# Batch 5's exponentials moved one batch earlier and summed on GpSimd, in an attention and gated-FFN kernel

## The chip, the cores and the metric

One core of a Trainium2 chip. A time is the device time in microseconds (us) of one execution of the whole program. Engines are named as in the profile: PE is TensorE (PEld its weight loads), DVE is VectorE, ACT is ScalarE, POOL is GpSimd, SP is SyncE, which only issues transfers here.

## What is computed

Eight batches of attention with 8 heads, 576 positions and a head size of 64, compressed to 32 memory slots, and then a gated feed-forward block over all 4608 tokens:

```python
a = np.exp(phi - np.max(phi, axis=2, keepdims=True))          # phi: (8, 8, 576, 32)
a = a / (np.sum(a, axis=2, keepdims=True) + 1e-09)
k_m = np.einsum('bhsm,bhsd->bhmd', a, k)
v_m = np.einsum('bhsm,bhsd->bhmd', a, v)
scores = scale * np.matmul(q, k_m.transpose(0, 1, 3, 2))
attn = softmax(scores)                                         # over the 32 slots
x = np.matmul(attn, v_m)   # -> (4608, 512)
g = x @ w_gate             # 512 x 1536
out = (g * (1.0 / (1.0 + np.exp(-g))) * (x @ w_val)) @ w_out   # 1536 x 512
```

The change concerns the first two lines for one batch: the exponentials of phi and their sum over the 576 positions, the denominator of each of the 8 x 32 memory slots.

## The kernel before

All matmuls are in bfloat16 with float32 sums. The order of instructions on each engine is the order in which the program is written (a manual schedule); an engine takes its instructions one after the other and waits on semaphores. Batches 0 and 1 are a prologue; a loop runs over `b` from 2 to 7. One turn of the loop has two parts.

*Attention of b.* TensorE works off a backlog of output products of the batch before, six matmul units at a time (`run(take(6))`), and between them the scores of b (L396) are made. The products follow a seven-product scheme: four blocks of the hidden layer and their sums (`t_S`) are multiplied with blocks of the output weights and their sums (`t_T`), so that seven block products replace eight. They run in the order first, five, six, three, seven, four (L822), each with 12 matmuls (two per unit), and they accumulate in three PSUM banks called "s", "a" and "c" (in the profile p_os, p_oa, p_oc). Where a bank's sum is needed by itself and goes on being added to, `keep` (L744 to L750) copies it to SBUF on ScalarE: p5 from "c" (tile t_p) and q6 from "s" (tile t_q; the batch's q has a tile of the same name). ScalarE also takes the exponentials of the scores (L407) and, in the same stretch because the exponential's table is loaded there, the exponentials of the next batch's phi: `phi_exp(b + 1)` (L172, tile t_ephi, one instruction over 128 x 1152 elements). DVE computes the normalisation (L435 to L452) and writes the normalised attention t_A. Then ScalarE loads the table for silu (L1042).

*Gates of b.* TensorE makes 24 gate and 24 value products (L515, p_g and p_v), ScalarE the silu (L532), DVE the product of the two (L538, tile t_h). GpSimd makes sums of t_h (L603, L560, t_S), for the output products. Interleaved with the gates, TensorE prepares batch b + 1: the denominators (L258), the sums of k and v weighted by the exponentials (L230), and the values times the gate weights (L472).

The denominators go in one of two ways. `kv_denominators` multiplies with a matrix of ones either the nine blocks of t_ephi (nine products of 128 x 128 by 128 x 2), or, where `esums` has an entry for the batch, a high and a low bfloat16 part of their sum (two products). The sum is made by `phi_sum` on GpSimd at the head of the gates: it waits for the attention of the running batch through a one-element copy (`wait_for`, L645, t_mark), so that it doesn't start earlier, then does four additions (L212), a cast (L218) and a subtraction (L219). Batches 3, 4, 6 and 7 have such sums; batch 5 doesn't, since in the gates of batch 4 GpSimd works on `quad_sums(0)` (sums of the leftover rows of batches 0 to 3). In `kv_items`, a batch with sums other than 3 takes its denominators behind the k and v sums; batch 3, and batch 5 with its nine products, takes them ahead of these in a PSUM bank of their own (p_S).

Loads: `loads(b)` issues q, phi, k and v of batch b on GpSimd's queue, in this order. It is called for b + 3 from the gates of b, when the second of three chunks of t_h is done (`chunk_done`, L633). So the loads of batch 5 are issued in the gates of batch 2, and two phi tiles take turns. `load_qT` (SyncE's queue) then transposes q by a transfer, for batch 5 in the gates of batch 4.

The lines that fix the place of the exponential and of the sum in one turn of the loop, cut:

```python
        run(take(6))                # product five, ends with the copy p5
        if not last:
            phi_exp(b + 1)
        z_inv_v(b, 1)
        ...
        run(take(6))                # product six, ends with the copy q6
        run_late()
        ...
        nc.scalar.preload_act_table_set("silu_and_others")
        run(take(6))                # product three
        ...
        run(take(6))                # product seven
        ...                         # then the gates:
            if b != 4:
                phi_sum(b + 1)
```

Of the kernel before, what the change touches and what calls it, by code (L numbers as in the profile page):

```python
# [10 lines left out]
BF16 = mybir.dt.bfloat16  # L11
# [3 lines left out]
def kernel(  # L15
# [19 lines left out]
    nc = tc.nc  # L35
# [20 lines left out]
    att = ctx.enter_context(tc.tile_pool(name="att", bufs=2))  # L56
# [18 lines left out]
    def bank(shape, dtype, name):  # L75
        tag = free.pop(0)
        t = ps.tile(shape, dtype, tag=tag, name=name)
        held[id(t)] = tag, t
        return t

    def done(*tiles):

        for t in tiles:
            free.append(held.pop(id(t))[0])
# [3 lines left out]
    def head_pairs(x):  # L88

        return x.rearrange("h s d -> (h s d)").rearrange("(i p f) -> p i f", i=NP, p=128)  # L90

    def load_phi(b, eng):
        t = inp.tile([128, NP, JK * M], FP32, tag="phi", name="t_phi")
        eng.dma_start(out=t, in_=head_pairs(phi[b]))
        phis[b] = t
# [6 lines left out]
    def load_v(b):  # L102
        nc.gpsimd.dma_start(out=kvs[b][:, 1], in_=head_pairs(v[b]))  # L103

    def load_q(b):

        t = inp.tile([128, NS * 128], BF16, tag=f"q{Q_SLOT[b]}", bufs=1, name="t_q")
        nc.gpsimd.dma_start(  # L108
            out=t,
            in_=q[b].rearrange("h s d -> (h s d)").rearrange("(p f) -> p f", p=128),  # L110
        )
        qs[b] = t
# [55 lines left out]
    ephis, rSs, bkvs, kTs, es, atts = {}, {}, {}, {}, {}, {}  # L168

    def phi_exp(b):  # L170
        t = att.tile([128, JK, NP, M], BF16, tag="ephi", name="t_ephi")
        nc.scalar.activation(  # L172
            out=t.rearrange("p j i m -> p i j m"),
            in_=phis.pop(b).rearrange("p i (j m) -> p i j m", m=M),
            func=AF.Exp,
        )
        ephis[b] = t
# [24 lines left out]

    esums = {}

    def phi_sum(b):

        e = ephis[b].rearrange("p j i m -> p j (i m)")
        wait_for(atts[b - 1, 1][0:1, 0, 0:1])  # L210
        t = att.tile([128, 4, 128], FP32, tag="es", bufs=1, name="t_es")
        add = lambda o, x, y: nc.gpsimd.tensor_tensor(out=o, in0=x, in1=y, op=ALU.add)  # L212
        add(t, e[:, 0:4], e[:, 4:8])
        add(t[:, 0:2], t[:, 0:2], t[:, 2:4])
        add(t[:, 0], t[:, 0], t[:, 1])
        add(t[:, 0], t[:, 0], e[:, 8])
        hl = att.tile([128, 2, 128], BF16, tag="ehl", bufs=1, name="t_ehl")
        nc.gpsimd.tensor_copy(out=hl[:, 0], in_=t[:, 0])  # L218
        nc.gpsimd.tensor_tensor(out=hl[:, 1], in0=t[:, 0], in1=hl[:, 0], op=ALU.subtract)  # L219
        esums[b] = hl  # L220
# [18 lines left out]
    def kv_denominators(b, p):  # L239

        if b in masked:
            for g in range(NG):
                for j in range(JK):
                    nc.tensor.matmul(
                        p[:, g:g + 1],
                        lhsT=masked[b][:, j, g].rearrange("p i m -> p (i m)"),
                        rhs=ones1,
                        start=(j == 0),
                        stop=(j == JK - 1),
                    )  # L250
            return
        if b in esums:
            hl = esums.pop(b)
            terms = [hl[:, t] for t in range(2)]
        else:
            terms = [ephis[b][:, j].rearrange("p i m -> p (i m)") for j in range(JK)]
        for n, x in enumerate(terms):
            nc.tensor.matmul(p, lhsT=x, rhs=ones2, start=(n == 0), stop=(n == len(terms) - 1))  # L258

    def kv_reciprocal(b, p):  # L260
        r = att.tile([128, NG], FP32, tag="rS", name="t_rS")
        nc.vector.reciprocal(out=r, in_=p)
        rSs[b] = r
# [28 lines left out]
    def kv_items(b, beside=None):  # L292


        def run_sums():
            o = 2 * D
            behind = b in esums and b != 3
            own = beside and not behind
            if own:
                d = bank([128, NG], FP32, "p_S")  # L300
                kv_denominators(b, d)
                kv_reciprocal(b, d)
                done(d)
            p = [bank([128, CH], FP32, f"p_kv{g}") for g in range(NG)]
            if not (own or behind):
                kv_denominators(b, p[0][:, o:o + NG])
            kv_sum(b, p, (0, 1))
            if behind:
                beside()
                kv_denominators(b, p[0][:, o:o + NG])  # L310
            if not own:
                kv_reciprocal(b, p[0][:, o:o + NG])
            kv_norm(b, p)
            if beside and not behind:
                beside()

        return [run_sums, lambda: kv_T(b)]
# [324 lines left out]
    def wait_for(x):  # L642

        t = att.tile([1, 1], BF16, tag="mark", bufs=1, name="t_mark")
        nc.gpsimd.tensor_copy(out=t, in_=x)  # L645
# [331 lines left out]
    def loads(b):  # L977

        if b < B:
            load_q(b)  # L980
            load_phi(b, nc.gpsimd)
            load_k(b)
            load_v(b)

# [6 lines left out]
    for b in range(2, B):  # L991
        last = b + 1 == B
        exp_tables()
        if b == 2:
            load_qT(3)
            phi_exp(2)
            (zero, ops0), (one, ops1) = products(0, ("c11",)), products(1, ("p1", "c11"))
            kv, q2 = kv_items(2), q_items(2, "aaa")
            run(zero[:6])
            sums = {n: f for n, f in zip(((1, 1), (0, 2), (1, 2)), late)}  # L1000
            late.clear()
            sums[0, 2]()
            weight_sums(0)
            weight_sums(1)
            run(zero[6:12] + one[:6] + kv[:1] + q2[:2])
            weight_sums(2, (0, 1))
            run(zero[12:16] + q2[2:] + zero[18:22] + kv[1:] + zero[16:18] + zero[22:24])
            weight_sums(2, (2, 3))
            ops0["c11"]()
            ops1["p1"]()  # L1010
            wait_for(Ts[2][0:1, 3, 0, 0:1])
            for part in ((0, 1), (3,), (2,)):
                for c in (1, 2):
                    sums[1, c](part)
            loads(4)
            backlog = one[6:12] + zero[36:] + one[12:36]
            ops = ops1
        else:
            run(take(6))
        for g in range(NG):  # L1020
            scores(b, g)
        if b > 2:
            ops["p1"]()
            u_values(b)
        else:
            run(zero[24:36] + take(6))
        run(take(6))
        z_inv_v(b, 0)
        ops["c11"]()
        run(take(6))  # L1030
        if not last:
            phi_exp(b + 1)
        z_inv_v(b, 1)
        if b > 2:
            norm(b, 0)
            norm(b, 1)
        run(take(6))
        run_late()
        if b == 4:
            wait_for(atts[4, 1][0:1, 0, 0:1])  # L1040
            quad_sums(0)
        nc.scalar.preload_act_table_set("silu_and_others")  # L1042
        run(take(6))
        if b == 2:
            norm(2, 0)
        run(take(6))
        if b == 2:
            norm(2, 1)
            u_three(2)
            run(one[36:])  # L1050
        g = gv_slots(b)
        quad = []
        if b == 4:
            quad = products(b, (), 0)[0]
        if last:
            rest, rest_ops = products(b, (), 1)
            backlog += rest[:12]
        beside = 0 if last else 2 if quad else min(4, len(backlog))
        outs = [lambda: run(take(1)) for _ in range(len(backlog) - beside)]
        streams = [(g, 0, 24), (quad[:12], 0, 3), (quad[12:], 12, 18.5)]  # L1060
        streams += [(outs, 4, 7 if quad else 24)]
        if b == 2:
            streams += [([lambda: u_values(2)], 2.5, 3)]
        if last:
            streams += [([u_item(b, 2)], 5, 6)]
        if not last:
            if b > 2:
                load_qT(b + 1)
            if b != 4:
                phi_sum(b + 1)  # L1070
            streams += [
                (kv_items(b + 1, lambda: (u_item(b, 2, "aava")(), run(take(2)))), KV, KV + 4),
                ([lambda: (u_three(b + 1), run(take(2)))], 19, 20),
            ]
        spread(*streams)
        flush_mul()
        units, ops = products(b, ("p1", "c11"))
        backlog += units
# [34 lines left out]
```

## Time and profile before

| what | value |
|---|---|
| median of 3 runs | 232.76 us (232.63 to 233.4) |
| the profiled execution | 232.59 us, of which the span from first to last instruction is 230.8 us |
| granted TensorE clock in it | 1.0 |
| busy, share of the span | PE 96%, PEld 74%, DVE 80%, ACT 74%, POOL 63% |
| exponentials of phi on ScalarE (L172) | 6 of 1.16 to 1.17 us; batch 4's starts at 96.07 us, batch 5's at 119.92 us |
| denominators (L258) of batch 5 | 9 products from 128.53 us on |
| first sums of GpSimd in the gates of batch 3 | from 99.22 us on |
| loads of batch 5 | issued from 91.20 us on |

Times in the profile count from the first instruction. A line of a timeline gives the start, the duration, the engine, the line of the kernel, the operation, the tile written and those read, the shapes and how many instructions of a kind were merged; a bracket gives idle time of the engine before it and what ended it. Matmuls are pipelined, so their durations overlap: the distance from start to start is what one costs. "Landing" of a transfer is counted from the start of its issue.

### The profile page before, as it was taken

The numbers are of one execution on the slowest core, as the hardware profiler recorded it, in microseconds if no ns is written. First come the engines' busy times: TensorE is split into PE (matmuls) and PEld (weight loads), VectorE is DVE, ScalarE is ACT, GpSimd is POOL, SyncE is SP. The second block draws the span as 40 slices with busy tenths as digits, with TensorE's granted clock in tenths as the row PEclk, the third lists the DMA queues.
The fourth block names the chain that finished last, engine by engine and source line by source line (L and its number), as shares of the span: only waits on it lengthen the run. The fifth ranks groups of instructions, "written<-read, shape, count | busy, mean of one in ns | idle before, by whom it ended". The sixth has DMA issues, their size and how long they took to land.

```text
span 230.8 us, 7191 instructions
## 1 busy us (share of the span) xinstructions
PE 222.3 (96%) x2818; PEld 169.7 (74%) x2818; DVE 184.8 (80%) x423; ACT 171.6 (74%) x365; POOL 145.1 (63%) x197
## 2 busy tenths in 40 slices
PE   6997799999999999999999999999999999999993
PEld 2554476778887777878788787887788778878882
DVE  4056789999976799989997668998999899977832
ACT  2858898988547989968896658978898789677310
POOL 8422427998099759765977689464845394029291
PEclk9999999999999999999999999999999999999999
DMA  6999999999996993999299964996022602202024
GB/s 213 209 211 206 199 207 207 216 250 266 207 210 176 258 257 69 224 204 177 78 214 195 230 137 110 253 231 101 18 76 102 116 0 95 87 7 91 23 93 162
DMA packets 36546, 36.84 MB, mean 160 GB/s; under 512 B 14496, under 2 KB 30880, under 8 KB 36512
## 3 DMA queue, kind: packets, MB, share of 16 engines
q0 software_dynamic: 16272, 22.42, 52.7%
q1 hardware_dynamic: 19712, 13.37, 22.8%
q10 hardware_dynamic: 528, 0.59, 0.8%
q8 instruction: 22, 0.36, 0.6%
q14 instruction: 12, 0.10, 0.1%
HBM read 42.47 MB, written 9.44 MB: 225 GB/s over the span
## 4 chain that ended last, share of the span: by engine, by line
PE 87%; DMA 9%; POOL 2%; issue 0%; DVE 0%; POOLq 0%
PE p_os L723 21%; PE p_g L515 21%; PE p_v L515 20%; PE p_oc L723 10%; DMA W<-in_moe_w_val_dram 9%; PE p_oa L723 5%; PE p_u L472 5%; PE p_kv L230 2%; PE p_g L396 1%; POOL t_kv L99 1%; POOL t_kv L103 1%; PE p_q L383 1%; POOL t_q L108 0%; POOL W L138 0%; DVE t_q L339 0%
## 5 line engine op out<-in xcount | busy, mean ns | idle before, releaser
L538 DVE TENSOR_TENSOR t_h<-t_sg,p_v 128x288 bf16<-128x288 bf16 x192 | 81.7, 451 | 14.3 <-PE p_v L515 7.3
L515 PEld LDWEIGHTS <-t_U 128*128 128x128 bf16 x768 | 73.9, 98 | 21.2 <-issue 3.5
L532 ACT ACTIVATE t_sg<-p_g 128x288 bf16<-128x288 f32 x192 | 73.2, 424 | 17.2 <-PE p_g L515 11.4
L515 PE MATMUL p_g<-t_A,t_U 128*128 128x288 bf16 x384 | 77.0, 286 | 0.0
L515 PE MATMUL p_v<-t_A,t_U 128*128 128x288 bf16 x384 | 76.9, 286 | 0.0
L723 PEld LDWEIGHTS <-t_S 128*128 128x128 bf16 x384 | 37.3, 98 | 4.5 <-issue 0.2
L603 POOL TENSOR_TENSOR t_S<-t_h 128x512 bf16<-128x512 bf16 x17 | 19.6, 1154 | 27.7 <-DVE t_h L538 26.4
L723 PEld LDWEIGHTS <-t_h 128*128 128x128 bf16 x288 | 27.1, 98 | 8.6 <-issue 5.0
L492 ACT CAST t_U<-p_u 128x512 bf16<-128x512 f32 x51 | 27.0, 606 | 6.4 <-PE p_u L472 6.4
L723 PE MATMUL p_os<-t_T,t_S 128*128 128x256 bf16 x192 | 23.7, 273 | 0.0
L560 POOL TENSOR_TENSOR t_S<-t_S,t_h 128x512 bf16<-128x512 bf16 x17 | 19.6, 1155 | 1.3
L560 POOL TENSOR_TENSOR t_S<-t_h 128x512 bf16<-128x512 bf16 x16 | 18.4, 1152 | 0.0
L560 POOL TENSOR_TENSOR t_S<-t_h,t_S 128x512 bf16<-128x512 bf16 x16 | 18.4, 1151 | 0.0
L472 PE MATMUL p_u<-W,t_kT 64*32 64x512 bf16 (+1 forms) x416 | 15.3, 363 | 1.2 <-DMA W<-in_moe_w_val_dram 0.6
L870 PE MATMUL p_warm<-bones 128*128 128x512 bf16 x44 | 13.6, 450 | 1.7 <-DVE bones L892 1.7
L496 DVE CAST t_U<-p_u 128x512 bf16<-128x512 f32 x21 | 13.6, 683 | 1.9 <-PE p_u L472 1.9
L723 PE MATMUL p_os<-t_T,t_h 128*128 128x256 bf16 x96 | 14.8, 273 | 0.0
L452 DVE TENSOR_TENSOR t_A<-t_E,t_lz 128x576 bf16<-128x576 bf16 x16 | 11.4, 739 | 0.7 <-ACT t_lz L428 0.7
L723 PE MATMUL p_oc<-t_T,t_S 128*128 128x256 bf16 x96 | 11.9, 273 | 0.0
L723 PE MATMUL p_oa<-WO,t_h 128*128 128x256 bf16 x96 | 11.8, 273 | 0.0
L723 PE MATMUL p_oc<-WO,t_S 128*128 128x256 bf16 x96 | 11.8, 273 | 0.0
L723 PE MATMUL p_os<-WO,t_h 128*128 128x256 bf16 x96 | 11.8, 273 | 0.0
(108 smaller groups left out, 312.5 us busy)
## 6 DMA issues: line engine op xcount, KB each, us to landing
out_dram<-t_o SPq DMA_DIRECT2D x11, 512.0 KB, 3.3
t_kv<-in_k_dram POOLq DMA_DIRECT2D x8, 576.0 KB, 10.7
t_q<-in_q_dram POOLq DMA_DIRECT2D x8, 576.0 KB, 8.7
t_kv<-in_v_dram POOLq DMA_DIRECT2D x8, 576.0 KB, 15.1
t_phi<-in_phi_dram POOLq DMA_DIRECT2D x6, 576.0 KB, 8.5
out_dram<-t_o SPq DMA_DIRECT2D x10, 256.0 KB, 3.8
WO<-in_moe_w_out_dram POOLq DMA_DIRECT2D x3, 512.0 KB, 19.4
W<-in_moe_w_gate_dram POOLq DMA_DIRECT2D x2, 512.0 KB, 16.5
```

The source lines that it names most:

```text
L230: nc.tensor.matmul(p[g][32 * i:32 * i + 32, 0:n], lhsT=phi_of(b, g, j, i), rhs=kvs[b][64 * g:64 * g + 64, w0:w1, i, j * D:(j + 1) * D], st ...
L452: nc.vector.tensor_tensor(out=a, in0=es.pop((b, g)), in1=lzs.pop((b, g)), op=ALU.mult)
L472: nc.tensor.matmul(p[g][32 * i:32 * i + 32, o:o + n], lhsT=kTs[b][64 * g:64 * g + 64, 2, 32 * i:32 * i + 32], rhs=w_part(w, c, i, g, halve ...
L492: nc.scalar.copy(out=t, in_=p)
L496: nc.vector.tensor_copy(out=t, in_=p)
L515: nc.tensor.matmul(p[:, 0:HALF], lhsT=Us[b, c, g][:, o // 2, which, 128 * (o % 2):128 * (o % 2 + 1)], rhs=atts[b, g][:, r], start=(g == 0) ...
L532: nc.scalar.activation(out=sg, in_=gate[:, 0:HALF], func=AF.Silu)
L538: nc.vector.tensor_tensor(out=dst, in0=sg, in1=val[:, 0:HALF], op=ALU.mult)
L560: eng.tensor_tensor(out=out, in0=x, in1=y, op=ALU.subtract)
L603: eng.tensor_tensor(out=t[:, 0], in0=A21, in1=A22, op=ALU.add)
L723: nc.tensor.matmul(mine[home][:, u], lhsT=lhs(c, m, u), rhs=rhs(c, m), start=fresh and u == 0, stop=(k == 5), skip_group_check=u == 1 or n ...
L870: nc.tensor.matmul(p[:, 0:128 * a], lhsT=bones, rhs=x.to_broadcast([128, a, 128]) if a > 1 else bones, start=True, stop=True,)
```

## The change

The loop takes the exponentials of batches 4 and 5 in the attention of batch 3, one after the other, and none in the attention of batch 4. In the gates of batch 3 GpSimd makes the sums for batch 4 and then those for batch 5; both wait for the attention of batch 3 (`before`). The high and low parts get two buffers instead of one. Batch 5 keeps its place for the denominators (ahead of the k and v sums, in a bank of its own), which the test in `kv_items` now has to say, and takes two products there instead of nine. In the loads of batch 5, phi is issued ahead of q.

```diff
-    def phi_sum(b):
+    def phi_sum(b, before):
         e = ephis[b].rearrange("p j i m -> p j (i m)")
-        wait_for(atts[b - 1, 1][0:1, 0, 0:1])
+        wait_for(atts[before, 1][0:1, 0, 0:1])
...
-        hl = att.tile([128, 2, 128], BF16, tag="ehl", bufs=1, name="t_ehl")
+        hl = att.tile([128, 2, 128], BF16, tag="ehl", name="t_ehl")
...
         def run_sums():
             o = 2 * D
-            behind = b in esums and b != 3
+            behind = b in esums and b not in (3, 5)
...
     def loads(b):
         if b < B:
+            if b == 5:
+                load_phi(b, nc.gpsimd)
             load_q(b)
-            load_phi(b, nc.gpsimd)
+            if b != 5:
+                load_phi(b, nc.gpsimd)
             load_k(b)
             load_v(b)
...
         if not last:
-            phi_exp(b + 1)
+            for n in {3: (4, 5), 4: ()}.get(b, (b + 1,)):
+                phi_exp(n)
         z_inv_v(b, 1)
...
-            if b != 4:
-                phi_sum(b + 1)
+            for n in {3: (4, 5), 4: ()}.get(b, (b + 1,)):
+                phi_sum(n, b)
```

## The prediction

> **What bounds the kernel now.** I read the page first, for the engine that ends the run; then the timelines of ScalarE and TensorE around the place where the moved exponential lands (attention of batch 3); then TensorE at the denominators, GpSimd in the gates of batch 3, and the DMA issues ahead of the moved load.
>
> The page: busy time by engine, the granted clock, the chain that ended last.
>
> ```profile
> PE 222.3 (96%) x2818; PEld 169.7 (74%) x2818; DVE 184.8 (80%) x423; ACT 171.6 (74%) x365; POOL 145.1 (63%) x197
> PEclk9999999999999999999999999999999999999999
> PE 87%; DMA 9%; POOL 2%; issue 0%; DVE 0%; POOLq 0%
> ```
>
> TensorE carries 87% of the chain at a full clock, and the DMA part is the weight load at the start, which the change doesn't touch. From batch 2 on the program is a TensorE stream without holes: a window from 91.0 to 152.0 us shows it busy for all 61.0 us. So time taken out of that stream is won, and a hole put into it is lost; work on the other engines counts only where TensorE ends up waiting for it.
>
> ScalarE in the attention of batch 3 (start, duration, engine, line, operation):
>
> ```profile
> 95.59 0.58 ACT L748 COPY t_p<-p_oc 128x512 f32<-128x512 f32 x1 [0.26 <-PE p_oc L723]
> 96.07 1.17 ACT L172 ACTIVATE t_ephi<-t_phi 128x1152 bf16<-128x1152 f32 x1
> 97.14 0.58 ACT L748 COPY t_q<-p_os 128x512 f32<-128x512 f32 x1
> 97.73 1.28 ACT L1042 ACT_TABLE_LOAD   x1
> 99.77 0.41 ACT L532 ACTIVATE t_sg<-p_g 128x288 bf16<-128x288 f32 x1 [0.75 <-PE p_g L515]
> ```
>
> TensorE in the same stretch:
>
> ```profile
> 95.39 1.47 PE L723 MATMUL p_os<-t_T,t_S 128*128 128x256 bf16 x12
> 96.70 1.47 PE L723 MATMUL p_oc<-WO,t_S 128*128 128x256 bf16 x12
> 98.01 1.47 PE L723 MATMUL p_os<-t_T,t_S 128*128 128x256 bf16 x12
> 99.32 0.65 PE L515 MATMUL p_g<-t_A,t_U 128*128 128x288 bf16 x4
> ```
>
> These two belong together. The p_os of 95.39 is product six, the p_oc of 96.70 product three, the p_os of 98.01 product seven. Six and seven share one PSUM bank ("s"): `keep("q6", "s")` copies six out on ScalarE (t_q, 97.14 to 97.72) and only then may seven add into the bank. Today the copy ends 0.29 us before seven is due at 98.01. The exponential of L172 stands directly ahead of that copy in ScalarE's order.
>
> TensorE at batch 5's denominators (nine products, then the sums of k and v), and at batch 3's, which already has two products and the same bank of its own (p_S):
>
> ```profile
> 128.53 0.37 PE L258 MATMUL p_S<-ones,t_ephi 128*128 128x2 bf16 x9
> 128.83 0.80 PE L230 MATMUL p_kv<-t_kv,t_ephi 64*32 64x128 bf16 x72
> ...
> 79.84 0.19 PE L258 MATMUL p_S<-ones,t_ehl 128*128 128x2 bf16 x2
> 79.96 0.80 PE L230 MATMUL p_kv<-t_kv,t_ephi 64*32 64x128 bf16 x72
> ```
>
> Nine products hold the stream for 128.83 - 128.53 = 0.30 us, two for 79.96 - 79.84 = 0.12 us.
>
> GpSimd, from the loads of batch 5 to the first sums of batch 3's gates:
>
> ```profile
> 91.20 0.58 POOL L108 DMA_DIRECT2D t_q<-in_q_dram  x1
> 91.78 0.77 POOL L94 DMA_DIRECT2D t_phi<-in_phi_dram  x1
> ...
> 99.22 0.18 POOL L645 COPY t_mark<-t_A 1x1 bf16<-1x1 bf16 x1 [2.39 <-DVE t_A L452]
> 99.36 1.15 POOL L212 TENSOR_TENSOR t_es<-t_ephi 128x512 f32<-128x512 bf16 x1
> ...
> 102.79 0.43 POOL L219 TENSOR_TENSOR t_ehl<-t_es,t_ehl 128x128 bf16<-128x128 f32 x1
> 106.47 1.15 POOL L603 TENSOR_TENSOR t_S<-t_h 128x512 bf16<-128x512 bf16 x1 [3.25 <-DVE t_h L538]
> ```
>
> One phi_sum is 99.22 to 103.22, 4.0 us, and 3.25 us of idle follow it.
>
> DMA issues of that stretch (last number: us from issue to landing):
>
> ```profile
> t_q<-in_q_dram POOLq DMA_DIRECT2D x1, 576.0 KB, 5.4
> t_phi<-in_phi_dram POOLq DMA_DIRECT2D x1, 576.0 KB, 6.5
> ```
>
> Batch 5's q lands at 91.20 + 5.4 = 96.6, its phi at 91.78 + 6.5 = 98.3.
>
> **Part 1, seven products fewer.** Batch 5 goes from the p_S row with nine to the one with two: 0.30 - 0.12 = 0.18 us out of the stream, in the gates of batch 4. What follows (k and v sums, U, the casts on ScalarE at 129.89 that wait for TensorE) hangs on TensorE and moves along. Bounds: 0.18 gained, or nothing if a later wait eats it. I take 0.18. The two rows have weight loads of 95 to 98 ns each, yet the nine come about 25 ns apart.
>
> The Trainium skill, page "TensorE: Matmul & The Clock Gate", section "Back-to-back issue gap", says that small matmuls which each load weights are spaced by the weight load as well, about 81 ns at 128 columns; by that, as an estimate, seven products would be worth 0.57 us and the net below only +0.26. The nine products of this trace contradict it for this form, and I go by them.
>
> **Part 2, the second exponential.** It stands right behind the first, at 97.14, and takes ScalarE another 97.14 - 96.07 = 1.07 us from start to start. The copy t_q goes from 97.14 to 98.21 and ends at 98.79. Seven waits for it. A TensorE that stands waiting starts some 0.05 us after its releaser: DVE's copy of q ends at 13.00 + 1.23 = 14.23 and the waiting scores matmul starts at 14.28. So seven starts at 98.84 instead of 98.01: a hole of 0.83 us in the stream. Bounds: 0.78 with no release delay; 0.95 if the release takes three times as long.
>
> What stands behind the hole: gates of batch 3 move from 99.32 to 100.15. ScalarE's table load moves from 97.73 to 98.80 and ends at 100.08, while its first gate moves to 99.77 + 0.83 = 100.60, so the 0.75 us of idle there covers it. DVE's add that reads t_q (L753) starts at 99.01, after two norms, and finds t_q ready at 98.79. Everything later is paced by TensorE, so nothing gives the 0.83 back.
>
> In batch 4 the exponential is gone from ScalarE, but there the copy t_q (120.98 to 121.56) was in time for product seven at 121.85, and the first gate waits 0.97 us for TensorE: gain nothing.
>
> **Part 3, GpSimd.** The second phi_sum runs from 103.22 to about 107.2, where 3.25 us of idle were. The sums of batch 3 wait for t_h at 106.47, moved by the hole to 107.30: covered, cost nothing. Without the hole they would be 0.75 us late; the chain behind them has 0.37 us of idle at 117.33, and the last term that TensorE reads in batch 4 (ready at 119.69, read from 121.85) has over 2 us to spare. GpSimd at work beside DVE costs little: DVE's gate multiply takes 454 ns during the first phi_sum and 444 ns in the idle stretch after it, so perhaps four multiplies are 10 ns longer, 0.04 us at most and on an engine that TensorE does not wait for. The second mark waits for the same norm as the first, so it queues nothing new; the second ehl buffer removes a wait instead of adding one.
>
> **Part 4, the loads.** All four loads of batch 5 are still issued from 91.20 on. phi passes q: q lands no later than 98.3 instead of 96.6 and is wanted by the transposing load at 123.85, so it costs nothing; k and v keep their places. phi has to land before 97.14. First in the line, with q's 5.4 us from issue and 0.19 us more for its longer issue (0.77 against 0.58), it lands at 96.8 at the latest, 0.3 us in time; it moves half of q's source bytes, so sooner is likelier. Cost nothing, and one for one beyond 97.14.
>
> The Trainium skill, page "DMA: Bandwidth & Descriptors", section "Anatomy of one DMA — SWDGE (gpsimd) path", fits a GpSimd load as about 2.0 us plus bytes at 436 GB/s; as an estimate that is 3.4 us from the end of the issue and a landing at 95.3. The q row says up to 1.5 us later; by either the exponential is not held up and the sum stays.
>
> **Sum.** -0.18 + 0.83 = +0.65 us. On the profiled execution (span 230.8, time 232.59) that is 233.24; the median of the runs shown stands 0.17 higher at 232.76, and on it the forecast is 233.4.
>
> **The rivals.**
> A, the copy is not what seven waits for (another order on ScalarE, or slack that the trace doesn't show): only Part 1 is left, 232.6 on the median. For it speaks that the trace shows no wait of TensorE for t_q; against it that the slack is just 0.29 us and 1.07 us are put ahead of it on the same engine.
> B, clearly slower: phi of batch 5 lands late. If it lands at 98.3 as it does today, the exponential starts at 98.3 instead of 97.14, and the copy, product seven and all behind them move by another 1.2 us: +1.8 us, 234.6. It decides from 97.14 on; a landing at 97.5 would be +1.0. For it: the first packets of a set flow thinly for over a microsecond. Against: q, with twice the source bytes, lands at 96.6 from that place.
> C, the denominators stay nine: kv_denominators looks only at whether batch 5 has sums, so this would need the sums not to be built; 1% or so, and it would leave +0.83.
>
> **How the numbers follow.** Main case 80%: net between +0.60 (0.78 - 0.18) and +0.95 (the long release, nothing of Part 1 kept). About 0.3%, 0.70 us, is what a measurement of this kernel can tell from no change, and it cuts through this case: below it lie the sums that keep the 0.18, above it those that lose it; since the hole can hardly shrink while the gain can be lost, 37% below and 43% above. B 8%, slower. A 10%: 8% no difference, 2% faster. Of the remaining 2%, where ScalarE's relief in batch 4 is worth something that I can't see, I make faster too. Together faster 4%, same 45%, slower 51%. The range goes from A's side, 232.5, to B's landing at 97.9 (+1.4), 234.2.
>
> **What would show it.** After the change: two rows of L172 one behind the other near 96.1 and 97.1, t_q<-p_os near 98.2, and a hole of 0.8 us on TensorE ahead of the third p_os of batch 3, which the list of waits would give as L723 waiting for ScalarE's t_q L748; nine L258 rows on t_ephi left instead of eighteen; phi_sum twice back to back with the idle of 3.25 us gone. Wrong would be: seven still starting 1.31 us after three; or idle ahead of the second L172 ended by the DMA of t_phi.

## The result, and the profile after

The changed kernel takes 233.39 us (median of 20 runs, 233.22 to 234.32) against 232.69 us of the kernel before, timed beside it (20 runs, 232.44 to 233.4). The ratio is 1.0034, 95% interval 1.0027 to 1.0041: slower by 0.6 to 1.0 us. The profiled execution took 233.22 us with a span of 231.4 us; beside the profile of before that is 233.22 - 232.59 = +0.63 us.

The page after, the same three lines as before:

```profile
PE 222.1 (96%) x2811; PEld 169.3 (73%) x2811; DVE 185.1 (80%) x423; ACT 172.0 (74%) x365; POOL 148.9 (64%) x204
PEclk9999999999999999999999999999999999999999
PE 86%; DMA 9%; POOL 2%; ACT 1%; issue 1%; DVE 0%; POOLq 0%
```

Seven matmuls fewer on PE (2811 for 2818), seven instructions more on POOL (204 for 197: the six of a phi_sum and its mark), and ACT, which was not on the chain at all, now holds 1% of it. The busy lines alone would not tell that the kernel got slower: PE, the bound, has 0.2 us less work. What rose is its idle time.

ScalarE's timeline in the attention of batch 3, after:

```profile
95.59 0.59 ACT L748 COPY t_p<-p_oc 128x512 f32<-128x512 f32 x1 [0.26 <-PE p_oc L723]
96.08 2.22 ACT L172 ACTIVATE t_ephi<-t_phi 128x1152 bf16<-128x1152 f32 x2
98.20 0.57 ACT L748 COPY t_q<-p_os 128x512 f32<-128x512 f32 x1
98.79 1.28 ACT L1046 ACT_TABLE_LOAD   x1
100.57 1.64 ACT L532 ACTIVATE t_sg<-p_g 128x288 bf16<-128x288 f32 x4 [0.50 <-PE p_g L515]
```

TensorE's timeline in the same stretch, after:

```profile
95.39 1.47 PE L723 MATMUL p_os<-t_T,t_S 128*128 128x256 bf16 x12
96.70 1.47 PE L723 MATMUL p_oc<-WO,t_S 128*128 128x256 bf16 x12
98.82 1.47 PE L723 MATMUL p_os<-t_T,t_S 128*128 128x256 bf16 x12 [0.64 <-ACT t_q L748]
100.13 0.65 PE L515 MATMUL p_g<-t_A,t_U 128*128 128x288 bf16 x4
```

The copy t_q starts at 98.20 instead of 97.14, and product seven (the p_os of 98.82) now carries a bracket that it didn't have before: it waited for ACT's t_q. The bracket says 0.64, but the loss is 98.82 - 98.01 = 0.81 us: the bracket counts only from the modelled end of the last matmul, and matmuls overlap, so distances from start to start are what to read. The gates follow at 100.13 instead of 99.32.

The denominators of batch 5, after (the two rows of the k and v sums give the pace):

```profile
129.34 0.19 PE L258 MATMUL p_S<-ones,t_ehl 128*128 128x2 bf16 x2
129.46 0.80 PE L230 MATMUL p_kv<-t_kv,t_ephi 64*32 64x128 bf16 x72
```

129.46 - 129.34 = 0.12 us in place of 0.30. Laid start to start beside the trace of before, TensorE's stream is level to within 0.05 us from 27 us on until product seven, 0.81 us late from there on, and 0.63 us late from the k and v sums of batch 5 to the end of the program. There is no third step. (Ahead of 27 us lie the prologue's waits for loads, which end some tenths earlier or later from one execution to the next; they are level again by 27 us.)

GpSimd from the loads of batch 5 to the first sums of batch 3's gates, after:

```profile
91.21 0.79 POOL L94 DMA_DIRECT2D t_phi<-in_phi_dram  x1
92.00 0.55 POOL L108 DMA_DIRECT2D t_q<-in_q_dram  x1
...
103.17 0.18 POOL L645 COPY t_mark<-t_A 1x1 bf16<-1x1 bf16 x1
103.31 1.16 POOL L212 TENSOR_TENSOR t_es<-t_ephi 128x512 f32<-128x512 bf16 x1
...
107.28 1.16 POOL L603 TENSOR_TENSOR t_S<-t_h 128x512 bf16<-128x512 bf16 x1
```

The second phi_sum fills what was idle time, and the sums of batch 3 start at 107.28 with no idle ahead of them: they were due at 106.47 + 0.81. The DMA issues of that stretch, after:

```profile
t_phi<-in_phi_dram POOLq DMA_DIRECT2D x1, 576.0 KB, 4.3
t_q<-in_q_dram POOLq DMA_DIRECT2D x1, 576.0 KB, 6.2
```

phi landed at 91.21 + 4.3 = 95.5, 1.6 us before its exponential. In the traces of the experiments that load phi first it took 4.4 to 4.9 us and landed between 95.7 and 96.2, so at least 0.9 us ahead of 97.14.

### The profile page after: what moved, and what is told of

Read it like the earlier page. It is cut to its first block, busy times and chain, and to the rows that moved or that the text cites. A ratio compares the mean times of both kernels' runs of the same rounds, so it can differ in the third digit from the quotient of the medians.

```text
span 231.4 us, 7184 instructions
## 1 busy us (share of the span) xinstructions
PE 222.1 (96%) x2811; PEld 169.3 (73%) x2811; DVE 185.1 (80%) x423; ACT 172.0 (74%) x365; POOL 148.9 (64%) x204
## 4 chain that ended last, share of the span: by engine, by line
PE 86%; DMA 9%; POOL 2%; ACT 1%; issue 1%; DVE 0%; POOLq 0%
PE p_g L515 21%; PE p_v L515 20%; PE p_os L723 20%; PE p_oc L723 10%; DMA W<-in_moe_w_val_dram 9%; PE p_oa L723 5%; PE p_u L472 5%; PE p_kv L230 2%; ACT t_ephi L172 1%; PE p_g L396 1%; POOL t_kv L99 1%; POOL t_kv L103 1%; PE p_q L383 1%; POOL t_q L108 0%; POOL W L138 0%
## 5 line engine op out<-in xcount | busy, mean ns | idle before, releaser
L603 POOL TENSOR_TENSOR t_S<-t_h 128x512 bf16<-128x512 bf16 x17 | 19.7, 1156 | 24.5 <-DVE t_h L538 22.9
L560 POOL TENSOR_TENSOR t_S<-t_S,t_h 128x512 bf16<-128x512 bf16 x17 | 19.6, 1156 | 1.3
L560 POOL TENSOR_TENSOR t_S<-t_h,t_S 128x512 bf16<-128x512 bf16 x16 | 18.4, 1153 | 0.0
L560 POOL TENSOR_TENSOR t_S<-t_h 128x512 bf16<-128x512 bf16 x16 | 18.4, 1153 | 0.0
```

Source lines behind the costliest of these rows:

```text
L560: eng.tensor_tensor(out=out, in0=x, in1=y, op=ALU.subtract)
L603: eng.tensor_tensor(out=t[:, 0], in0=A21, in1=A22, op=ALU.add)
```

## The experiments

All take the changed kernel as their base, or the version of the first experiment, and were timed beside the kernel before.

### The exponential behind the copy

```diff
-        if not last:
-            for n in {3: (4, 5), 4: ()}.get(b, (b + 1,)):
-                phi_exp(n)
+        if not last and b != 4:
+            phi_exp(b + 1)
         z_inv_v(b, 1)
         ...
         run(take(6))              # product six, ends with the copy q6
+        if b == 3:
+            phi_exp(5)
         run_late()
```

> The changed kernel with one thing moved: batch 5's exponential stands behind the copy t_q (q6) on ScalarE in the attention of batch 3, not ahead of it. Sums on GpSimd, order of the loads and the two denominator products stay. Theory (the copy behind the second exponential holds product seven): t_q goes from 97.14 again, product seven starts at 98.01, no hole; the 0.18 us of the seven products stay won: 0.18 us under the kernel before, about 232.5, ratio 0.999. ScalarE's table load would end at 100.08, 0.31 us later than its first gate was due at 99.77; TensorE has free banks there, so I expect no wait of it. Rival (GpSimd's second phi_sum or the order of the loads costs the time, and the hole only lies where TensorE would have waited a little later anyhow): TensorE waits elsewhere in the gates of batch 3 or the attention of batch 4 and the time stays near +0.6 us.

Measured: 232.48 us (11 runs), ratio to before 0.999, interval 0.9981 to 0.9999. ScalarE, then TensorE, of this version:

```profile
96.15 1.17 ACT L172 ACTIVATE t_ephi<-t_phi 128x1152 bf16<-128x1152 f32 x1
97.21 0.58 ACT L748 COPY t_q<-p_os 128x512 f32<-128x512 f32 x1
97.68 1.18 ACT L172 ACTIVATE t_ephi<-t_phi 128x1152 bf16<-128x1152 f32 x1
98.87 1.28 ACT L1047 ACT_TABLE_LOAD   x1
100.17 1.80 ACT L532 ACTIVATE t_sg<-p_g 128x288 bf16<-128x288 f32 x5
```

```profile
96.78 1.47 PE L723 MATMUL p_oc<-WO,t_S 128*128 128x256 bf16 x12
98.08 1.47 PE L723 MATMUL p_os<-t_T,t_S 128*128 128x256 bf16 x12
99.39 0.65 PE L515 MATMUL p_g<-t_A,t_U 128*128 128x288 bf16 x4
```

Product seven follows three without a hole, and the gates follow seven. (Everything in this trace lies 0.07 us later than in the trace of before from 27 us on, behind the prologue's waits for loads; the distances count. From the denominators of batch 5 on it lies 0.10 us earlier, a gain of 0.17 us.) The first silu starts some 0.3 us after its gate was ready, right behind the table load, and TensorE doesn't notice. GpSimd's first sums start at 107.19, 0.65 us later than their operands were ready in the kernel before, and no wait of TensorE comes of it either. So the second phi_sum, the order of the loads and the later table load are free; the whole loss of the change is where the exponential stands. This version beats both kernels. Against before the medians differ by 0.30 us (the interval reaches from 0.02 to 0.44), the traces by the 0.17 us of the denominators.

### Nine products again, hole kept

```diff
-            for n in {3: (4, 5), 4: ()}.get(b, (b + 1,)):
+            for n in {4: ()}.get(b, (b + 1,)):
                 phi_sum(n, b)
```

> The changed kernel without the sums of batch 5 on GpSimd: the exponential stays moved, phi is still loaded first, and batch 5's denominators are nine products again. Theory: the hole ahead of product seven stays at 0.81 us and the 0.18 us of the denominators are not won: 0.8 us above the kernel before, 0.18 above the changed one, ratio about 1.0035. Rival (GpSimd's second phi_sum costs something): less than +0.6 us.

Measured: 233.67 us (5 runs), ratio 1.0037, interval 1.0024 to 1.0051. The median is 0.89 us above before; 0.81 was expected and lies in the interval, as do smaller values down to 0.56, so the times alone don't separate it from the changed kernel. The trace does: product three starts at 96.75 and seven at 98.87, the same hole of 0.81 us (98.87 - 96.75 - 1.31), and the nine products run from 129.73 to the k and v sums at 130.03, 0.30 us. So without the second phi_sum the hole is as long as with it. The profiled execution (233.79, the longest of the five) also has a second hole, in the gates of batch 3, with nothing that the profile could name as its cause:

```profile
105.38 0.41 PE L515 MATMUL p_v<-t_A,t_U 128*128 128x288 bf16 x2
105.97 0.42 PE L515 MATMUL p_g<-t_A,t_U 128*128 128x288 bf16 x2 [0.18 <-issue]
```

From start to start that is 0.59 instead of 0.25, 0.34 us lost. No other run's trace has it at this place. It says how far one profiled execution can be trusted where tenths matter, and is why the seven products were tested once more, in the fifth experiment.

### phi loaded second

```diff
     def loads(b):
         if b < B:
-            if b == 5:
-                load_phi(b, nc.gpsimd)
             load_q(b)
-            if b != 5:
-                load_phi(b, nc.gpsimd)
+            load_phi(b, nc.gpsimd)
```

> The changed kernel with the loads of batch 5 in the order of before: q, then phi. Theory: phi lands at about 98.3 (91.78 + 6.5) instead of 95.5, the second exponential starts there instead of at 97.14, the copy t_q ends at about 99.95 and the hole ahead of product seven grows from 0.81 to about 2.0 us: +1.8 us against before. Rival (ScalarE has slack there that the trace doesn't show): the hole stays at 0.8 us.

Measured: 234.61 us (2 runs), ratio 1.008, interval 1.0062 to 1.0098: +1.8 us. phi landed 6.6 us after its issue. ScalarE and TensorE of this version:

```profile
98.42 1.16 ACT L172 ACTIVATE t_ephi<-t_phi 128x1152 bf16<-128x1152 f32 x1 [1.19 <-DMA t_phi<-in_phi_dram]
99.49 0.57 ACT L748 COPY t_q<-p_os 128x512 f32<-128x512 f32 x1
```

```profile
96.70 1.47 PE L723 MATMUL p_oc<-WO,t_S 128*128 128x256 bf16 x12
100.11 1.47 PE L723 MATMUL p_os<-t_T,t_S 128*128 128x256 bf16 x12 [1.94 <-ACT t_q L748]
```

ScalarE now stands 1.19 us for the transfer, and the hole is 100.11 - 96.70 - 1.31 = 2.10 us. A wait on ScalarE passes to TensorE in full; the turned order of the loads in the change is what kept this from happening.

### One exponential more

```diff
         nc.scalar.activation(out=..., in_=..., func=AF.Exp)
+        if b == 5:
+            nc.scalar.activation(out=..., in_=..., func=AF.Exp)    # the same again
```

> The changed kernel with batch 5's exponential taken twice in a row into the same tile: one suspected cost doubled, nothing else. Theory: each exponential ahead of the copy t_q costs its 1.07 us from start to start one for one, so the hole ahead of product seven is 0.81 + 1.07 = 1.88 us and the time +1.7 us against before. The table load then ends at 101.15 and the gates start at 101.2, so it could add up to 0.1 us. Rival (part of the hole is a fixed cost of the wait, not the length of the exponential): the hole grows by clearly less or more than 1.07 us.

Measured: 234.51 us (2 runs), ratio 1.0076, interval 1.0057 to 1.0094: +1.7 us. ScalarE of this version (the lines behind the added exponential are numbered 7 higher in it):

```profile
96.19 2.22 ACT L172 ACTIVATE t_ephi<-t_phi 128x1152 bf16<-128x1152 f32 x2
98.44 1.16 ACT L178 ACTIVATE t_ephi<-t_phi 128x1152 bf16<-128x1152 f32 x1
99.51 0.57 ACT L755 COPY t_q<-p_os 128x512 f32<-128x512 f32 x1
```

TensorE's product three starts at 96.82 and seven at 100.13: a hole of 100.13 - 96.82 - 1.31 = 2.00 us, 1.19 more than with two exponentials. I had said 1.07. The third starts at 98.44, after the pair's end at 98.41, while independent ones overlap by 0.1 us (96.08 and 98.20 in the changed kernel hold two at 1.06 each). The third writes the tile that the second writes, and that it therefore waits for the second's end is inferred; the trace names no wait there. The second thus stands 1.18 us ahead of the third's start, and the hole grows by about that: what goes ahead of the copy costs its distance to the next start, and no fixed part shows.

### Sums made but not read

On the version of the first experiment:

```diff
-        if b in esums:
+        if b in esums and b != 5:
             hl = esums.pop(b)
```

> The version with batch 5's exponential behind the copy t_q, with GpSimd's sums for batch 5 still made but not read: batch 5's denominators are nine products again. It takes the two products away and leaves everything else. Theory (the gain of 0.18 us is the seven products and nothing else, and the sums, the loads and the later exponential are free): the time of the kernel before, ratio 1.000, and the denominators take 0.30 us of TensorE's stream again. Rival (the gain comes from ScalarE's relief in batch 4 or from the order of the loads): it stays 0.18 us or more under the kernel before.

Measured: 232.66 us (11 runs), ratio to before 0.9996, interval 0.9986 to 1.0005; 0.18 us above the first experiment's 232.48 us. TensorE at batch 5's denominators in this version:

```profile
128.66 0.37 PE L258 MATMUL p_S<-ones,t_ephi 128*128 128x2 bf16 x9
128.96 0.76 PE L230 MATMUL p_kv<-t_kv,t_ephi 64*32 64x128 bf16 x67
```

0.30 us again, and laid beside the first experiment's trace the stream falls 0.18 us behind exactly here and nowhere later. The seven products are the whole gain; the interval of either time taken alone would not show so small a thing, the step in the trace does.

### The two products behind the sums

On the version of the first experiment:

```diff
-            behind = b in esums and b not in (3, 5)
+            behind = b in esums and b != 3
```

> The version with batch 5's exponential behind the copy t_q, and batch 5's two products behind the sums of k and v like those of batches 4, 6 and 7, in the bank of the sums, not ahead of them in a bank of their own. Two products behind the sums took 0.06 us of the stream in batch 4 (104.22 to 104.28) against 0.12 us ahead of them in batch 3 (79.84 to 79.96). Theory: another 0.06 us, 0.24 us under the kernel before, ratio 0.999. Rival: DVE's reciprocal then comes later (behind the products instead of beside the sums), so the copies of the sums and their banks come later, and in the crowded gates of batch 4 TensorE waits for a bank: 0.1 to 0.3 us slower than the version without this.

Measured: 232.85 us (11 runs), ratio 1.0001, interval 0.9992 to 1.001: 0.37 us above the first experiment, the rival's direction and a little beyond its 0.1 to 0.3 us. Nor did the stretch of the sums get shorter: from the product ahead of them to the first gate behind them (128.34 to 130.35 here, 128.39 to 130.35 in the first experiment) the stream takes 2.01 us against 1.96, and in the gates that follow it falls another 0.35 us behind. TensorE, then DVE, of this version:

```profile
130.35 0.41 PE L515 MATMUL p_g<-t_A,t_U 128*128 128x288 bf16 x2
130.84 0.41 PE L515 MATMUL p_v<-t_A,t_U 128*128 128x288 bf16 x2
...
131.33 0.41 PE L515 MATMUL p_v<-t_A,t_U 128*128 128x288 bf16 x2
131.82 0.41 PE L515 MATMUL p_g<-t_A,t_U 128*128 128x288 bf16 x2
```

```profile
129.93 0.69 DVE L496 CAST t_U<-p_u 128x512 bf16<-128x512 f32 x1 [0.86 <-PE p_u L472]
130.54 0.16 DVE L262 RECIPROCAL t_rS<-p_kv 128x2 f32<-128x2 f32 x1
130.73 0.99 DVE L266 TENSOR_SCALAR t_bkv<-p_kv,t_rS 128x128 bf16<-128x128 f32 x4
131.64 2.37 DVE L538 TENSOR_TENSOR t_h<-t_sg,p_v 128x288 bf16<-128x288 bf16 x5
```

At two places (130.35 to 130.84 and 131.33 to 131.82) a pair of matmuls takes 0.49 us from start to start, instead of 0.28 and 0.24 in the first experiment. DVE copies the sums (L266) only from 130.73 on, because the reciprocal waits for the products; with the products ahead it does so from 129.58, while TensorE is still at other work. In this version DVE's first gate multiply behind them starts at 131.64, against 131.15. That TensorE stands for a bank which DVE has not freed is inferred from this order; the trace names no releaser for the two steps. Whatever the cause, the time speaks for the place ahead of the sums that the change keeps for batch 5's denominators.

### The sum for batch 5 made twice

On the version of the first experiment:

```diff
-            for n in {3: (4, 5), 4: ()}.get(b, (b + 1,)):
+            for n in {3: (4, 5, 5), 4: ()}.get(b, (b + 1,)):
                 phi_sum(n, b)
```

> The version with batch 5's exponential behind the copy t_q, with GpSimd's six instructions for batch 5's sum done twice: 3.95 us more on GpSimd, nothing else. In the version without this GpSimd runs without idle time from 99.3 to 118.9, so all 3.95 us pass on: the third sum of chunk 1 (made from 117.83 to 118.97) is ready at about 122.9 instead of 118.97. Product three of batch 3 reads it at its third unit, at about 120.8. Theory (GpSimd is hidden only by a cover of about 2 us in front of the products of batch 3): TensorE stands about 2.1 us ahead of that unit, and the time is about 234.6, +1.9 us against before. Rival (GpSimd has more room than that, or its sums are not what TensorE reads): the time stays at 232.5.

Measured: 234.81 and 236.38 us (2 runs; the second is the profiled one), ratio 1.012, interval 1.0081 to 1.016. TensorE of the profiled one:

```profile
120.52 0.60 PE L723 MATMUL p_oc<-WO,t_S 128*128 128x256 bf16 x4
123.31 1.89 PE L723 MATMUL p_oc<-WO,t_S 128*128 128x256 bf16 x8 [2.19 <-POOL t_S L560]
```

The third unit of product three was due four matmuls after the first, at 120.52 + 4 x 0.11 = 120.96, and started at 123.31: 2.35 us lost to the sum that GpSimd (L560, 122.11 + 1.14) had ready at 123.25. In the version with the single sum the same sum is ready at 117.83 + 1.15 = 118.98 and that unit starts at 121.06: the cover that hides GpSimd in batch 3 is 2.1 us there. The delay that used it up, 123.25 - 118.98 = 4.27 us, is larger than the 3.9 us that the doubled sum adds: GpSimd's three instructions from 116.00 on, which now stood beside sums on DVE (last section), took 3.14 us up to the next issue of a load, against 2.71 us in the first experiment. The run of 234.81 us is what the hole makes of 232.48; the other run lost 1.6 us more, which is told there too.

## Why the prediction was right

The forecast was 233.4 us with a net of +0.65; measured were 233.39 us, and +0.63 in the profile. That the time agrees to 0.01 us is luck: the forecast stood on the median of three runs of before, 232.76, which is 0.07 us above that of the 20 runs timed beside the change, and the medians differ by 0.70. The mechanism is what was right: the same two steps, at the places that were named, and no third.

- *Part 2, the second exponential*: 0.83 us forecast, 0.81 measured in the trace, at the instruction that was named and with the releaser that was named. The release delay is the forecast 0.05 us (the copy ends at 98.77, seven starts at 98.82); the difference of 0.02 is that the exponentials stand 1.06 us apart instead of 1.07 and the copy takes 0.57 instead of 0.58. The first experiment took the hole away by the order on ScalarE alone; the third and fourth made it grow with whatever is ahead of the copy.
- *Part 1, seven products*: 0.18 forecast, 0.18 measured, and the fifth experiment shows that nothing else contributes. The estimate of 0.57 us from the Trainium skill's page "TensorE: Matmul & The Clock Gate", section "Back-to-back issue gap", is not what these products cost: the nine come 25 ns apart with their weight loads. The page gives its 81 ns for products with 128 moving columns, and its table of single products has a floor of about 25 ns for 1 to 64 columns; these have 2, so the estimate took the wrong row.
- *Part 3, GpSimd*: free, as said, with the hole and without it. The margin was argued from the term that product seven reads; the last experiment shows TensorE waiting for product three's first, and in the first experiment's trace that one is the tightest, with 2.1 us. There, with GpSimd without a pause, product three's term is ready at 118.98 and read at 121.06, product seven's, the next sum that GpSimd makes, at 120.10 and read at 122.37, which leaves 2.3 us. The conclusion stood, the row behind it was not the one with the least room. The 10 ns allowed for each of DVE's gate multiplies did not appear either: the three that took 441 to 446 ns in the stretch without GpSimd took 443 to 446 ns beside the second phi_sum.
- *Part 4, the loads*: free, as said, with phi at 95.5. The bound from q's row (96.8) was 1.3 us too late; the estimate from the Trainium skill's page "DMA: Bandwidth & Descriptors", section "Anatomy of one DMA — SWDGE (gpsimd) path", 95.3, was the nearer of the two in this trace. The landings of the other traces with phi first, 95.7 to 96.2, lie between them. Rival B's price, +1.8 us, is what the third experiment measured with the loads turned back.
- *Rival A* (the copy is not what seven waits for) is refuted by the bracket on seven, and by the first experiment, which takes the hole away. *Rival C* didn't happen.
- *The cut at 0.3%* ran through the main case as said: +0.63 in the profile is 0.27%, the ratio of the runs 0.34%, and its interval reaches to both sides of 0.3%.

## What to carry to other kernels

Where, as here, an engine fed without holes is the bound, a piece of work moved on another engine does not cost its length as such, its place decides: look for the small instruction behind it that the bound waits for, and take the slack from the distance between the end of the one and the start of the other (here 0.29 us against 1.07 us put in front). Moving it one instruction further, behind that copy, turned a loss of 0.63 us into a gain of 0.17, by the traces. And a load that is consumed earlier than before has to be checked against its landing, not only its issue: without the turned order this change would have lost 1.8 us.

## What the runs showed of the hardware

Two things, both in the profiled run of the last experiment. The hole of TensorE cost more than its length there: the matmuls directly behind it came 0.21 us apart instead of 0.11, and the windows of that run show the clock beside them (stretch, its length, busy time and instructions of PE, PEld, DVE, ACT and POOL, granted clock, DMA share, GB/s):

```profile
120.50:123.30 2.80, 0.62 (x6) 0.30 (x4) 2.73 (x5) 1.87 (x2) 2.80 (x5) 0.99 0.93 155
123.30:126.80 3.50, 3.49 (x18) 2.51 (x19) 3.18 (x4) 0.00 (x0) 2.80 (x5) 0.52 1.07 283
126.80:130.00 3.20, 3.20 (x30) 2.73 (x28) 1.44 (x3) 1.51 (x4) 3.20 (x7) 1.00 1.18 183
```

For 3.5 us after the hole the granted clock was 0.52, which cost 1.6 us on top of the hole; the other run of the same kernel, 1.57 us shorter at a mean clock of 0.998 against 0.993, fits a hole without it. The traces with holes of 2.00 and 2.10 us (fourth and third experiment) kept a mean clock of 0.999. The Trainium skill, page "TensorE: Matmul & The Clock Gate", section "What's actually happening", lets the clock drop after an idle window of about 3.4 us that runs freely; here a stand of 2.2 us by the bracket was followed by the drop, in one run of two. What decides between the two runs stays open.

And work on GpSimd and sums on DVE that read two tiles from SBUF got in each other's way. DVE's sums of chunk 2 of batch 3 (L560, two inputs in SBUF) in the timeline of before, where GpSimd was issuing transfers at that time:

```profile
116.17 0.42 DVE L560 TENSOR_TENSOR t_S<-t_S,t_h 128x512 bf16<-128x512 bf16 x1
116.51 0.42 DVE L560 TENSOR_TENSOR t_S<-t_h 128x512 bf16<-128x512 bf16 x1
```

and in the last experiment, where GpSimd's own sums (L603 and L560) had slipped beside them:

```profile
116.34 1.26 DVE L560 TENSOR_TENSOR t_S<-t_S,t_h 128x512 bf16<-128x512 bf16 x1
117.53 1.37 DVE L560 TENSOR_TENSOR t_S<-t_h 128x512 bf16<-128x512 bf16 x1
...
116.00 1.32 POOL L603 TENSOR_TENSOR t_S<-t_h 128x512 bf16<-128x512 bf16 x1
117.40 1.22 POOL L560 TENSOR_TENSOR t_S<-t_S,t_h 128x512 bf16<-128x512 bf16 x1
```

Three times as long on DVE; GpSimd's two took 1.15 to 1.16 us each in the first experiment. It is not this run alone: in the kernel before, the three sums of this form on DVE from 55.29 us on, beside copies on GpSimd (L592), took 0.64 to 0.66 us instead of 0.42. DVE's gate multiply, with one input in PSUM, shows nothing of the kind (441 to 446 ns without GpSimd, 443 to 446 ns beside the second phi_sum), so the second phi_sum, which lies in the gates, does no harm. The Trainium skill, page "SBUF — State Buffer", section "Who interferes with whom", says the same of the two forms: a DVE instruction with two SBUF inputs contends with a GpSimd instruction that reads SBUF, one with a single SBUF input outside certain modes doesn't. In the last experiment a delay on GpSimd grew in this way, from 3.9 to 4.3 us, once its sums were pushed out of their place.
